# A gated mix of sliding-window attention and a token-mixing MLP on one core: the written order of its five engines is replaced by another order of the same work

## The chip, the cores and the metric

The kernel runs on one core of one Trainium2 chip. The core has five engines that run side by side, each taking its own instructions in order: TensorE (PE, matrix products into the PSUM memory), VectorE (DVE), ScalarE (ACT), GpSimd (POOL) and SyncE (SP), which here only issues DMA transfers. The metric is the time of one execution on the device in microseconds; the number given is the median of several executions.

## The reference

There are 2048 tokens of width 512. Branch A is attention with 32 heads of width 16, in which a token sees itself and the 255 tokens before it. Branch B normalises each token and then mixes tokens: it multiplies along the token axis, 2048 to 1376 and back to 2048, for each of the 512 columns. A gate per token mixes the two.

```python
x = A_x
g = _sigmoid((x * gate_w).sum(-1, keepdims=True))
a = _A_ref(x, A_wqkv, A_wo)
b = _B_ref(x, B_w1, B_b1, B_w2, B_b2)
return g * a + (1 - g) * b

# in _A_ref, H = 32, Dh = 16, W = 256:
scores = jnp.einsum("bhqd,bhkd->bhqk", q, k) * (Dh ** -0.5)
mask = (idx[:, None] - idx[None, :] >= 0) & (idx[:, None] - idx[None, :] < W)
scores = jnp.where(mask[None, None], scores, -1e9)
p = _softmax(scores, axis=-1)
o = jnp.einsum("bhqk,bhkd->bhqd", p, v)
return (lambda x, *d: x.transpose(*d))(o, 0, 2, 1, 3).reshape(B, S, D) @ wo

# in _B_ref, F = 1376:
h = _layernorm(x, axis=-1)
u = jnp.einsum("bsd,sf->bdf", h, w1) + b1
u = _gelu(u)
y = jnp.einsum("bdf,fs->bds", u, w2) + b2
return (lambda x, *d: x.transpose(*d))(y, 0, 2, 1)
```

All inputs and the output are bf16; sums are kept in float32.

## The kernel before

The kernel is written as a list of tasks. A task is one or a few instructions of one engine with a name, the tasks it depends on, and the buffers it takes and uses. The function arrange then puts the tasks into the order in which they are issued. Which engine runs a task, and in which order each engine runs its tasks, is not computed there: it is read from the dictionary PLAN, which holds one written list of task names for each engine. A figure after a colon is the buffer a task takes: a PSUM bank for PE (0 to 7; two figures for a task that takes two pairs of banks), a scratch tile for the others. arrange walks down the five lists, always taking the head task that can start first by its own table of costs (cost_of, TURN, LATENCY). These costs set only how the five lists are woven into one, which projection or MLP product runs in 32-column pieces (the set THEN names tasks after which it does), and where a GpSimd instruction waits for VectorE because of a port that they share. In the program that is built, each engine simply runs its list; between engines there are waits where data or a PSUM bank is handed over.

The names, as PLAN writes them:

- x0.0, x0.2, x1.4, x2.8, x3.12 (line 489): loads of the rows of x, in four blocks of 512 tokens (block 0 in two halves). wqk0 to wqk3 (L505) and wv (L510): the projection's weights. gw (L542): the gate's weights. xt1 to xt3 (L498): loads of blocks 1 to 3 of x that transpose on the way. w1_gi (L521): weights of the first MLP product, group g of columns, tokens of block i. wo (L528), w2_f (L1315): weights of A's last product and of the second MLP product. vs, vz (L756 to L767): copies of V between partitions within SBUF. o0 to o15 (L1343): the output. All are issued by SP, on one queue.
- xta, xtc: block 0 of x transposed by PE (L646) and copied out (L640, L641). warm, warmb: matmuls on zeros ahead of the data (L626).
- k, q, v (all by chain, L708): projections; k2_1.0 is the first piece of K, part 2 of 4, block 1. kc, vc are their copies out of PSUM (ACT L640 or DVE L641), qc the copy of Q with a mask by parity (DVE L792).
- s3.v1, s3.C (L980, L1080, L1036): scores of query block 3. v0 to v3 cover the two key tiles that the window covers mostly, C its two corners. Each needs two pairs of PSUM banks.
- e3.v1.0 (ACT, L932): the exponentials of one of these pairs, 128 x 1024, into a tile et (or into a tile XT, once the transposed x is used up). m3.v1.0: zeros outside the window, by DVE (L1012, L945) or POOL (L571).
- pv3.0 to pv3.3 (L1125): products with V, and with a column of ones for the sum, into a pair of banks. n13, n23, nz3, n33, n43 (DVE, L1216, L1220, L1224, L1233, L1251): the transpose out of PSUM, reciprocal, factor with the gate, product, transpose back into the tile xo, for block 3.
- bs, ba (L808, L812), pow (POOL, L818), h (L824): the layer norm of one tile of 128 tokens. gl, gatem, gatee, ez: the gate.
- u0 to u10 (L708): first MLP product, 16 matmuls each; ub (ACT L473 or DVE L475): bias and copy into ug. gelu (ACT, L1291, L1293): gelu over all of ug at once, with a load of the function table before it, and one of the exponential's after it.
- y0 to y15 (L708): second MLP product and, in the last four matmuls, A's product with wo into the same bank. f (ACT L473, DVE L476) scales and adds the bias, o stores. y15 is cut into three parts l, m, r.

Branches A and B share PE from about 45 us on: u and later y tasks stand between the scores of A, while ACT works on exponentials. A chain of 2 full matmuls is

```python
last = add(
    f"{name}.{a}", {"PE": 0.2155 * sum(m[4] for m in mms[a:z]) / 512}, emit, d,
    takes=[b] if a == 0 else [], uses=([] if a == 0 else [b]) + list(also),
```

so its first piece takes the bank and waits until the last user of that bank has read it.

## Time and profile before

| | us |
|---|---|
| median of 3 runs | 199.56 (199.55 to 199.9) |
| profiled execution | 199.2 |
| its span, first to last instruction | 197.5 |
| TensorE busy | 187.4 (95%) |
| ACT busy | 169.9 (86%) |
| DVE busy | 157.8 (80%) |
| POOL busy | 64.6 (33%) |
| granted TensorE clock | 1.000 |

The profile is of one execution. Times inside it count from its first instruction. A line of the timeline gives the start, the length, the engine, the line of the kernel, the operation, what it writes and reads, how many instructions are merged into the line, and in brackets how long the engine was idle before and what ended that. PEld is TensorE's loading of weights, which overlaps its matmuls. "To landing" is the time from a transfer's issue to the signal that its last byte is there. Matmuls overlap, so the starts of two of them, not their lengths, show the pace.

### The profile page before, as it was taken

To read this page: it belongs to the slowest core of one execution; us is meant where nothing else is said; L and a number is where in the kernel's file an instruction comes from. 1 tells how busy PE (TensorE), PEld (TensorE's weight loads), DVE (VectorE), ACT (ScalarE), POOL (GpSimd) and SP (SyncE) were. 2 spreads that over 40 slices of the span, in tenths; PEclk is the share of its full clock that TensorE was granted. 3 is DMA by queue.
4 is the path that set the end of the run, shared out by engine and by line. 5 is a ranking of instruction groups with operands and counts; after the bars stand their busy time and mean duration, and the time that the engine had idled before them with its cause. 6 is when DMAs were issued, how large, how long until landed. Compare 5 with 4: busy or idle time off the path is not lost.

```text
span 197.5 us, 9026 instructions
## 1 busy us (share of the span) xinstructions
PE 187.4 (95%) x4008; PEld 92.3 (47%) x4040; DVE 157.8 (80%) x340; ACT 169.9 (86%) x200; POOL 64.6 (33%) x102
## 2 busy tenths in 40 slices
...
GB/s 147 306 212 125 236 328 346 317 123 63 7 156 69 275 62 37 0 3 36 134 391 256 3 39 211 0 5 56 3 109 36 27 9 68 3 3 89 3 98 65
DMA packets 23444, 22.01 MB, mean 111 GB/s; under 512 B 7950, under 2 KB 21518, under 8 KB 23406
## 3 DMA queue, kind: packets, MB, share of 16 engines
...
q14 instruction: 7, 0.06, 0.1%
...
## 4 chain that ended last, share of the span: by engine, by line
PE 79%; ACT 11%; DVE 4%; issue 3%; DMA 2%; SPq 0%; ACTq 0%
PE pb L708 57%; PE ps L1125 10%; PE ps L980 9%; ACT et L932 7%; PE ps L1080 2%; ACT VA L640 2%; DMA wqkv<-in_A_wqkv_dram 2%; DVE stats L808 1%; ACT L932 1%; DVE et L1216 1%; DVE zt L1233 0%; SPq L489 0%; ACT ug L1291 0%; DVE h L824 0%; PE ps L1036 0%
## 5 line engine op out<-in xcount | busy, mean ns | idle before, releaser
L932 ACT ACTIVATE et<-ps 128x1024 bf16<-128x1024 f32 (+1 forms) x104 | 98.8, 1011 | 8.2 <-PE ps L980 5.5
L571 POOL TENSOR_SCALAR_AFFINE_SELECT et<-et 128x512 bf16<-128x512 bf16 (+3 forms) x60 | 41.6, 704 | 98.4 <-ACT et L932 65.7
L932 ACT ACTIVATE XT<-ps 128x1024 bf16<-128x1024 f32 (+1 forms) x50 | 49.1, 1028 | 1.2 <-PE ps L980 0.7
L708 PEld LDWEIGHTS <-wb 128*32 128x32 bf16 (+4 forms) x663 | 32.5, 97 | 37.0 <-issue 7.0
L708 PE MATMUL pb<-ug,wb 128*32 128x512 bf16 (+6 forms) x344 | 43.9, 365 | 0.9 <-issue 0.6
L708 PE MATMUL pb<-h,wb 128*32 128x512 bf16 (+2 forms) x301 | 41.9, 380 | 1.7 <-issue 1.7
L708 PE MATMUL pb<-XT,wqkv 128*128 128x512 bf16 (+2 forms) x166 | 31.8, 369 | 1.2 <-issue 0.8
L980 PE MATMUL ps<-QZ,KT 32*128 32x256 bf16 (+1 forms) x496 | 23.1, 265 | 0.9 <-ACT et L932 0.8
L1125 PEld LDWEIGHTS <-VA 128*32 128x32 bf16 (+1 forms) x1056 | 20.3, 97 | 6.2 <-issue 1.6
L792 DVE TENSOR_TENSOR QZ<-pb,par 128x1024 bf16<-128x1024 f32 x16 | 19.1, 1213 | 3.3 <-PE pb L708 2.4
L1125 PE MATMUL ps<-et,VA 128*32 128x128 bf16 (+2 forms) x760 | 21.7, 217 | 0.0
L1216 DVE STREAM_TRANSPOSE et<-ps 128x1024 f32<-128x1024 f32 (+1 forms) x13 | 15.7, 1207 | 4.2 <-PE ps L1125 3.7
L1012 DVE TENSOR_TENSOR et<-et,mask 128x512 bf16<-128x512 bf16 x38 | 16.9, 454 | 2.7 <-ACT et L932 2.7
L708 PEld LDWEIGHTS <-wqkv 128*128 128x128 bf16 (+1 forms) x172 | 12.0, 97 | 13.7 <-DMA wqkv<-in_A_wqkv_dram 0.9
L571 POOL TENSOR_SCALAR_AFFINE_SELECT XT<-XT 128x512 bf16<-128x512 bf16 (+1 forms) x15 | 9.8, 659 | 24.5 <-ACT XT L932 13.5
L708 PE MATMUL pb<-wo,xo 128*32 128x512 bf16 (+3 forms) x152 | 17.5, 369 | 0.4 <-issue 0.3
L980 PEld LDWEIGHTS <-KT 32*128 32x128 bf16 x496 | 7.4, 92 | 21.7 <-ACT et L932 12.1
L708 PE MATMUL pb<-wqkv,XT 128*128 128x512 bf16 x60 | 15.8, 380 | 0.6 <-issue 0.3
L1012 DVE TENSOR_TENSOR XT<-XT,mask 128x512 bf16<-128x512 bf16 x20 | 9.7, 485 | 6.4 <-ACT XT L932 6.4
L808 DVE BATCH_NORM_STATS2 stats<-xo 128x6 f32<-128x512 bf16 x16 | 10.6, 675 | 4.2 <-DMA xo<-in_A_x_dram 4.2
L1125 PEld LDWEIGHTS <-VZ 128*32 128x32 bf16 x832 | 13.2, 97 | 0.4
L1125 PE MATMUL ps<-XT,VA 128*32 128x128 bf16 (+2 forms) x296 | 12.7, 217 | 0.1
...
## 6 DMA issues: line engine op xcount, KB each, us to landing
...
```

The costliest lines, as they stand in the source:

```text
L571: return nc.gpsimd.affine_select(out=out_, in_=in_, pattern=[[0, n] for n in pattern] + [[step, HB]], compare_op=op, fill=0.0, base=base_, ...
L640: return nc.scalar.activation(out_(), in_(), ACT.Copy)
L708: made.append(nc.tensor.matmul(buf(b)[c:z_, c0:c0 + w_], lhsT=lhsT[:, c:z_], rhs=rhs, start=(j == 0), stop=(j == n - 1), skip_group_check= ...
L792: lambda k=k, b=b: nc.vector.tensor_tensor(out=QZ[:, k, :, (i % NQ) * SB:(i % NQ + 1) * SB], in0=buf(b)[:, None, :].to_broadcast([P, 2, SB ...
L808: f"bs{t_}", {"DVE": 0.67}, lambda b=b, t_=t_: nc.vector.bn_stats(buf(b)[:], xo[:, t_, :]),
L932: lambda e=e, b=b, shape=shape: nc.scalar.activation(out=shape(buf(e)), in_=shape(buf(b)), func=ACT.Exp, scale=SCALE),
L980: made.append(nc.tensor.matmul(to[:, :, done:done + m], lhsT=keys(j if x == "A" else j - 1, k)[rows], rhs=q[rows], start=True, stop=True, ...
L1012: made.append(nc.vector.tensor_tensor(out=v, in0=v, in1=m.to_broadcast(list(v.shape)), op=ALU.mult))
L1080: made.append(nc.tensor.matmul(buf(b2[r // 2])[m_:m_ + HB, at:at + P], lhsT=keys(t_, k)[rows, a:a + HB], rhs=q[rows], start=True, stop=Tru ...
L1125: return lambda: nc.tensor.matmul(to(), lhsT=v() if callable(v) else v, rhs=buf(e)[rows, col:col + n], start=first, stop=last, tile_positi ...
L1216: lambda: nc.vector.transpose(out=view(buf(tr).bitcast(FP32)), in_=view(buf(o))), [last], takes=[tr], uses=[o],
```

## The change

All five lists of PLAN and the set THEN are replaced by others. The tasks are the same, 500 on PE and 74 on SP. Those that more than one engine can run are divided anew: ACT's list goes from 194 to 189 tasks, DVE's from 293 to 290, POOL's from 75 to 83. On ACT, ub0, ub1, ub6, ub10, vc13, kc1_1, kc1_2, kc3_3, f9, f12, f15r and one xtc are no longer run, and kc3_2, kc0_1, vc7, vc9, ub4, f10 and another xtc are. Two figures are changed besides: the cost of a score in cost_of, and the latency of the w2 loads, both of which arrange reads. The order was searched outside of the kernel; the description of the change says that this was done in the mean of three sets of durations, with loads and the blocks of TensorE's instructions in one queue of transfers. Nothing of that search is in the kernel.

```diff
@@ -91,7 +91,7 @@
 def cost_of(t, e):
     c, n = t.engines[e], t.name
     if e == "PE":
-        return c - 0.02 if t.mode == "s" else c * 0.738 if t.mode == "c" else c
+        return c - 0.01 if t.mode == "s" else c * 0.738 if t.mode == "c" else c
     if e == "DVE":
         return max(0.1, c - 0.06)
...
 
 PLAN = dict(
     PE="""
-        warm:5 xta0.0.1:4 xta0.0.0:3 warmb xta0.1.1:4 xta0.1.0:5 q2_0.0:6 q3_0.0:0 k1_0.0:2 k3_0.0:3
-        k0_0.0:1 q1_0.0:5 q1_0.1 k2_0.0:7 q0_0.0:4 k2_0.1 q2_0.1 k0_0.1 q0_0.1 k3_0.1 k0_0.2 q0_0.2 k1_0.1
-        q0_0.3 k3_0.2 q1_0.2 k3_0.3 q1_0.3 q3_0.1 q2_0.2 k1_0.2 q1_0.4 k1_0.3 q0_0.4 k0_0.3 k3_0.4 q2_0.3
-        k0_0.4 q3_0.2 q2_0.4 k2_0.2 k1_0.4 k2_0.3 k2_0.4 v1.0:1 q3_0.3 q3_0.4 s0.v0:24 v1.2 v0.0:7 q3_1.0:6
-        v0.2 q3_1.2 s0.C:24 v5.0:0 k2_1.0:7 k2_1.2 v5.2 s-1.C:24 v3.0:6 v14.0:7 v14.2 s1.v3:04 biast:3 v3.2
-        q1_1.0:7 q1_1.2 s1.v0:02 v2.0:6 v2.2 v12.0:4 v12.2 v4.0:5 v4.2 pv-1.0:0 s0.v1:26 k3_1.0:4 k3_1.2
-        k3_2.0:5 s1.v2:06 k3_2.2 v6.0:2 q0_1.0:3 q0_1.2 v6.2 pv0.0:0 pv0.1 pv0.2 s1.v1:46 v7.0:3 v7.2
-        v15.0:2 s2.v1:06 v15.2 k0_2.0:5 v13.0:4 k0_2.2 v13.2 k1_1.0:3 s1.C:06 k2_2.0:2 k2_2.2 k1_1.2
-        s2.v3:06 k0_1.0:5 k0_1.2 v10.0:2 v10.2 pv1.0:0 pv1.1 pv1.2 pv1.3 s2.v0:46 pv1.4 v8.0:2 v8.2 v9.0:3
-        v9.2 s2.v2:06 q2_1.0:5 k1_2.0:4 q2_1.2 s2.C:20 k1_2.2 u0.0:6 u0.2 v11.0:7 v11.2 s3.v1:40 u0.4 u0.6
...
-        u10.4 s8.v1:24 u9.6 u9.8 u10.6 u9.10 s8.v0:20 u9.12 u10.8 u9.14 s8.v2:42 u10.10 pv7.0:0 pv7.1
-        q1_3.0:6 u10.12 u10.14 q1_3.2 s10.v0:24 pv7.2 k2_3.0:7 k2_3.2 pv8.0:2 pv8.1 k0_3.0:6 pv8.2 pv8.3
-        pv7.3 k0_3.2 q2_3.0:4 q2_3.2 q3_3.0:5 y4.0:6 y0.0:7 q3_3.2 s9.v1:02 y0.2 y0.4 y4.2 y4.4 y0.6 y4.6
-        y0.8 y0.10 s9.v3:40 y0.11 y0.13 y4.8 s9.v2:02 y4.10 y4.11 y2.0:7 y2.2 s9.C:40 y2.4 y4.13 y2.6
...
-        y12.8 s15.A:04 y13.4 y13.6 y12.10 y12.11 y13.8 s15.C:02 y12.13 pv14.0:4 pv14.1 pv14.2 s15.B:20
-        y13.10 y13.11 pv14.3 y14.0:6 y14.2 y14.4 y15l.0:1 y13.13 y14.6 y14.8 pv15.0:4 pv15.1 pv15.2 y14.10
-        y15r.0:3 y15l.2 y15l.4 y14.11 y15r.2 y14.13 y15r.4 y15l.6 y15l.8 y15r.6 y15l.10 y15l.11 y15l.13
-        y15r.8 y15r.10 y15r.11 y15m.0:2 y15r.13 y15m.2 y15m.4 y15m.6 y15m.8 y15m.10 y15m.11 y15m.13
+        warm:6 xta0.0.1:7 xta0.0.0:3 warmb xta0.1.0:5 xta0.1.1:4 k3_0.0:1 k1_0.0:2 q2_0.0:3 q0_0.0:0 q2_0.1
+        k0_0.0:7 q0_0.1 q1_0.0:6 k3_0.1 q2_0.2 k1_0.1 q1_0.1 k2_0.0:5 k3_0.2 q0_0.2 q1_0.2 k2_0.1 k0_0.1
+        k0_0.2 k1_0.2 k3_0.3 q1_0.3 q0_0.3 k0_0.3 q0_0.4 k3_0.4 q1_0.4 q3_0.0:4 q2_0.3 k0_0.4 q3_0.1 k1_0.3
+        k2_0.2 q3_0.2 k1_0.4 k2_0.3 k2_0.4 q3_0.3 q3_0.4 q2_0.4 q3_1.0:2 s0.v0:60 q3_1.2 v1.0:5 v1.2 v0.0:4
+        v0.2 s0.C:06 v5.0:3 v5.2 k2_1.0:5 s-1.C:06 k2_1.2 v14.0:4 v14.2 s1.v3:02 v3.0:5 biast:7 v3.2
+        q1_1.0:4 q1_1.2 s1.v0:26 v12.0:5 v2.0:0 v2.2 v12.2 v4.0:1 v4.2 pv-1.0:2 s0.v1:46 k3_2.0:0 q0_1.0:1
+        q0_1.2 s1.v2:62 k3_2.2 k3_1.0:4 v6.0:5 k3_1.2 v6.2 pv0.0:0 pv0.1 pv0.2 s1.v1:26 k1_1.0:5 v7.0:4
+        k1_1.2 s2.v1:60 v7.2 v13.0:2 v10.0:3 v10.2 v13.2 k2_2.0:5 s1.C:06 k2_2.2 k0_2.0:3 k0_2.2 s2.v3:06
+        k0_1.0:4 v15.0:5 k0_1.2 v15.2 pv1.0:2 pv1.1 pv1.2 pv1.3 s2.v0:60 pv1.4 v9.0:5 k1_2.0:4 v9.2 k1_2.2
+        s2.v2:26 v8.0:1 q2_1.0:0 q2_1.2 v8.2 u0.0:2 s2.C:46 v11.0:3 v11.2 u0.2 s3.v1:06 u0.4 u2.0:3 u0.6
+        s3.C:40 u2.2 u0.8 u0.10 u0.12 u0.14 s3.v2:60 pv2.0:4 u2.4 pv2.1 pv2.2 pv2.3 u2.6 u2.8 s3.v0:60
...
+        u9.6 s8.v1:24 u9.8 u9.10 u10.4 u10.6 s8.v0:46 u9.12 u10.8 u9.14 s8.v2:24 u10.10 pv7.0:6 pv7.1 u10.12
+        u10.14 q1_3.0:0 q1_3.2 s10.v0:24 k0_3.0:1 k0_3.2 pv7.2 pv7.3 k2_3.0:4 k2_3.2 pv8.0:2 pv8.1 pv8.2
+        pv8.3 s9.v1:04 q3_3.0:6 q3_3.2 q2_3.0:7 y0.0:2 y4.0:3 q2_3.2 y4.2 y0.2 y0.4 y0.6 y4.4 y4.6 y0.8
+        y0.10 s9.v3:06 y4.8 y0.11 y0.13 y4.10 s9.v2:46 y4.11 y2.0:2 y2.2 s9.C:40 y2.4 y4.13 y2.6 s9.v0:46
...
+        pv13.1 pv13.2 pv13.3 s14.v1:24 y13.0:6 y13.2 y12.0:7 s14.C:40 y13.4 y12.2 y12.4 y12.6 s15.A:24 y12.8
+        y12.10 y13.6 y12.11 y12.13 s15.C:04 pv14.0:2 pv14.1 pv14.2 y14.0:7 pv14.3 s15.B:04 y13.8 y14.2
+        y13.10 y13.11 y14.4 y14.6 y14.8 y13.13 y14.10 pv15.0:4 pv15.1 pv15.2 y15l.0:3 y15l.2 y15r.0:2 y15r.2
+        y14.11 y15r.4 y15r.6 y15l.4 y15l.6 y14.13 y15l.8 y15l.10 y15l.11 y15l.13 y15r.8 y15m.0:1 y15r.10
+        y15r.11 y15m.2 y15r.13 y15m.4 y15m.6 y15m.8 y15m.10 y15m.11 y15m.13
     """,
     ACT="""
-        xtc0.0.1 xtc0.0.0 kc3_0 kc0_0 kc1_0 kc2_0 e0.v0.0:5 e0.v0.1:4 vc0 vc1 e0.C.0:3 e0.C.1:2 kc2_1 vc5
-        e-1.C.1:9 e-1.C.0:8 vc14 e1.v3.0:1 e1.v3.1:b e1.v0.0:a e1.v0.1:0 vc12 gatee0 vc4 e0.v1.1:8 e0.v1.0:9
-        e1.v2.0:6 e1.v2.1:7 kc3_1 vc6 e1.v1.1:2 e1.v1.0:3 e2.v1.1:4 e2.v1.0:5 vc15 kc0_2 e1.C.0:d e1.C.1:c
-        kc2_2 e2.v3.0:8 vc13 e2.v3.1:9 vc10 kc1_1 e2.v0.1:0 e2.v0.0:b vc8 e2.v2.0:1 e2.v2.1:7 e2.C.1:a kc1_2
...
-        e7.v3.1:b e7.C.1:e e7.C.0:7 e7.v2.1:9 e7.v2.0:h e8.v3.1:4 e8.v3.0:5 e8.C.1:c e8.C.0:d e8.v1.0:2
-        e8.v1.1:3 e8.v0.0:0 e8.v0.1:1 gatee3 e8.v2.1:8 e8.v2.0:a ub10 e10.v0.0:6 e10.v0.1:9 gelu e9.v1.0:8
...
-        e14.v1.0:j e14.C.1:5 e14.C.0:e e15.A.0:1 e15.A.1:0 e15.C.0:8 e15.C.1:3 f12:0 e15.B.0:2 e15.B.1:j
-        f13:3 f15r:1
+        xtc0.0.1 xtc0.1.0 kc3_0 kc1_0 kc0_0 kc2_0 e0.v0.1:6 e0.v0.0:7 vc1 e0.C.1:2 e0.C.0:3 vc0 vc5
+        e-1.C.0:9 kc2_1 e-1.C.1:0 vc14 e1.v3.1:8 e1.v3.0:1 e1.v0.0:b e1.v0.1:a vc12 gatee0 vc4 e0.v1.1:0
+        e0.v1.0:9 e1.v2.0:c kc3_2 e1.v2.1:d vc6 kc3_1 e1.v1.1:0 e1.v1.0:9 e2.v1.1:6 e2.v1.0:7 vc7 vc10
+        e1.C.0:4 e1.C.1:5 kc2_2 kc0_2 e2.v3.0:2 e2.v3.1:3 vc15 kc0_1 e2.v0.0:8 e2.v0.1:9 vc9 e2.v2.0:0
+        e2.v2.1:1 vc8 e2.C.1:b e2.C.0:a e3.v1.0:c e3.v1.1:d e3.C.1:e e3.C.0:f e3.v2.1:8 e3.v2.0:9 e3.v0.1:0
...
+        e7.v3.0:3 e7.v3.1:b e7.C.0:a e7.C.1:6 e7.v2.1:4 e7.v2.0:5 e8.v3.1:c e8.v3.0:e e8.C.0:d e8.C.1:f
+        e8.v1.1:8 e8.v1.0:9 e8.v0.0:g e8.v0.1:h e8.v2.0:0 e8.v2.1:1 gatee3 e10.v0.1:2 e10.v0.0:7 gelu
...
+        e14.v1.1:e e14.v1.0:j e14.C.0:a e14.C.1:f e15.A.1:i e15.A.0:7 e15.C.1:8 e15.C.0:9 e15.B.1:d
+        e15.B.0:b f13:3
     """,
     DVE="""
-        zeros bs0:0 ba0 bs3:1 const bs1:0 parity ba3 xtc0.1.0 xtc0.1.1 ba1 bs2:1 ba2 bs5:0 bs6:1 ba5 bs7:0
-        qc0_0 qc1_0 qc2_0 qc3_0 h1 gl3 qc3_1 h2 gl0 h3 ba7 gl1 gl2 biasc vc3 ba6 gatem0 qc1_1 bs4:0 vc2 ba4
-        bs11:1 bs8:0 n1-1:c ez0 ba8 kc3_2 bs10:0 qc0_1 ba10 n10:8 h5 ba11 n20 vc7 bs12:0 n2-1 h6 nz-1:1
-        nz0:0 n3-1:0 bs9:1 h7 m1.v1.0 ba9 n30:1 ba12 bs15:1 kc0_1 bs14:0 m1.C.0 ba14 ba15 bs13:0 ba13 n11:2
...
-        nz12:0 m13.v1.0 m14.v3.0 m13.v2.0 f11:3 n113:2 n312:0 m14.v2.1 m14.v2.0 n213 n412 m14.C.1 m14.v0.0
-        nz13:1 n313:1 m14.C.0 m14.v3.1 n413 m15.A.1 n114:g n214 nz14:1 n314:0 n414 n115:6 n215 nz15:0 n315:1
-        n415 f14:3 f15l:2 f15m:0
+        zeros bs0:1 bs1:0 xtc0.0.0 ba1 parity ba0 bs3:0 bs2:1 xtc0.1.1 ba2 ba3 const bs6:1 bs7:0 ba7 bs5:0
+        ba6 qc0_0 bs4:1 qc1_0 qc3_0 qc2_0 h1 gl7 ba5 h3 qc3_1 gl1 gl0 h0 m-1.C.0 ba4 biasc vc3 gl2 gl3 qc1_1
+        gatem0 vc2 n1-1:4 ez0 bs9:1 ba9 qc0_1 bs14:1 gl8 n10:2 n2-1 bs11:0 ba11 ba14 kc1_1 nz-1:0 n20 h2
+        n3-1:1 nz0:1 bs8:0 bs10:1 h5 n30:0 h6 ba10 vc13 ba8 m1.C.0 m1.C.1 bs15:0 bs13:1 ba15 m2.v3.1 h11
...
+        m13.C.0 n411 n112:g m13.C.1 n212 m13.v2.0 nz12:1 m13.v2.1 f6:2 f11:1 n113:8 n213 m14.v2.1 m14.v0.1
+        n312:1 m14.v0.0 m14.C.0 n412 nz13:0 m14.C.1 n313:1 m14.v1.1 f12:1 n413 n114:2 n214 m15.C.1 nz14:1
+        m15.A.0 n314:1 n414 n115:8 n215 nz15:0 n315:0 n415 f14:2 f15l:3 f15r:1 f15m:0
     """,
     POOL="""
-        ident masks ones blanks pow0 m0.v0.1 m0.v0.0 m-1.C.0 m-1.C.1 m0.C.1 pow1 m1.v3.1 m0.C.0 m0.v1.0
...
+        ident ones masks pow0 blanks m0.C.1 m-1.C.1 m1.v3.0 m0.v0.0 m0.C.0 m0.v0.1 pow1 m0.v1.1 m0.v1.0
+        m1.v2.0 m1.v2.1 m1.v3.1 m1.v0.0 m1.v0.1 m2.v1.0 m1.v1.1 m1.v1.0 pow2 m2.v3.0 m2.v1.1 pow3 m2.v0.1
...
     """,
     SP="""
-        x0.0 x0.2 wqk0 wqk1 wqk2 x1.4 wqk3 gw wv xt1 bias xt3 vs0 x2.8 vs1 xt2 w1_21 x3.12 w1_00 w1_01 w1_10
-        w1_02 w1_20 vs2 w1_23 w1_12 w1_11 vz4:1 w1_03 vz8:0 vz2:2 vz3:2 w1_13 w1_22 vz5:2 wo w2_0 w2_3 vz6:1
-        vz11:2 vz7:1 w2_1 w2_4 w2_2 w2_7 w2_6 w2_5 w2_8 vz10:0 w2_9 w2_10 vz9:1 o2 o4 o7 o0 o8 vz13:1 vz12:0
-        o5 o10 vs13 o1 o11 o9 vz14:1 o13 o3 o6 o12 o14 o15l o15r o15m
+        x0.0 x0.2 wqk0 wqk1 x1.4 wqk2 wqk3 xt1 wv gw xt3 bias x2.8 vs0 xt2 vs1 w1_00 vz2:0 x3.12 w1_01 w1_22
+        wo vs2 w1_12 w1_20 vz6:2 w1_10 w1_03 vz4:1 w1_02 w1_13 vz3:0 w1_21 w1_11 w2_1 w2_2 w1_23 vz5:0 w2_7
+        vz9:1 w2_6 vz8:0 w2_3 w2_5 vz7:2 w2_4 w2_8 w2_0 w2_10 w2_9 o4 vz11:2 vz10:0 o0 o8 o2 vz12:1 o5 o1
+        vs13 vz14:0 o10 o9 vz13:2 o6 o11 o7 o13 o12 o3 o14 o15l o15r o15m
     """,
 )
 
 THEN = set("""
-    pv-1.0 pv0.2 pv1.0 pv1.2 s2.v0 pv2.0 s3.v1 s3.v2 pv3.2 pv3.3 s4.v1 pv4.0 pv4.1 s5.v0 pv5.0 pv5.3 s6.v1
...
+    pv0.1 pv1.2 pv1.3 s2.v0 pv2.0 pv2.2 s3.v1 s3.v2 pv3.0 pv3.1 pv3.3 pv4.0 pv4.1 pv4.2 pv4.3 s5.v0 pv5.0
...
 """.split())
@@ -1312,7 +1311,7 @@
         gone = [piece[f"u{c}.{row // 2 * 2}"] for c in range(4 * g, min(4 * g + 4, NFC))]
         dw2.append(add(
             f"w2_{fc}", {"SP": 1.55 * fsz / P},
-            lambda fc=fc, fsz=fsz: nc.sync.dma_start(w2[:fsz, fc, :], B_w2[fc * P:fc * P + fsz, :]), gone, lat=2.9,
+            lambda fc=fc, fsz=fsz: nc.sync.dma_start(w2[:fsz, fc, :], B_w2[fc * P:fc * P + fsz, :]), gone, lat=3.2,
```

## The prediction

> **What bounds the kernel now.** I read the page's table of engines first, then the chain that ended last, then TensorE's own waits, and last the timeline of single stretches.
>
> ```profile
> PE 187.4 (95%) x4008; PEld 92.3 (47%) x4040; DVE 157.8 (80%) x340; ACT 169.9 (86%) x200; POOL 64.6 (33%) x102
> PE 79%; ACT 11%; DVE 4%; issue 3%; DMA 2%; SPq 0%; ACTq 0%
> ```
>
> TensorE (PE) is busy for 187.4 of 197.5 us and holds 79% of the chain. Matmuls overlap, so busy time alone doesn't say that PE runs at its pace; the starts do.
>
> ```profile
> 54.74 0.40 PE L980 MATMUL ps<-QZ,KT 32*128 32x256 bf16 x8
> 55.07 1.47 PE L708 MATMUL pb<-h,wb 128*128 128x512 bf16 x6
> 56.47 0.40 PE L980 MATMUL ps<-QZ,KT 32*128 32x256 bf16 x8
> 56.80 1.47 PE L708 MATMUL pb<-h,wb 128*128 128x512 bf16 x6
> 58.20 0.40 PE L980 MATMUL ps<-QZ,KT 32*128 32x256 bf16 x8
> ```
>
> Six full matmuls take 1.40 us from start to start (55.07 to 56.47): 6 x 0.216 and one change of tile shape of 0.10. Eight score matmuls take 0.33, 0.23 and another change. These paces hold wherever PE waits for nothing. I took the pace of each kind from the median distance of starts in this trace and added up the whole order of before from its first projection (5.82 us) to its last matmul (start 194.32). The sum is 186.86 us, the trace has 188.50: only 1.64 us of that stretch are waits. The rest of the span is 5.82 of start (limited by the first weights) and 3.17 after the last matmul starts (its output and the final store). So the work is a stream without gaps, and no order of the same work can gain more than about 1.6 us there.
>
> ```profile
> engine line waited for: us in total, times, longest us
> PE pb L708 <- issue: 3.8, 24, 0.2
> ...
> PE ps L980 <- ACT et L932: 0.8, 3, 0.4
> ```
>
> The 24 "issue" gaps are mostly single missing records (4040 weight loads against 4008 matmuls), not time. By starts, the 1.64 us lie at four places: 0.36 before the first scores, 0.83 between 29 and 43 us, 0.73 around 114 to 126, 0.15 at 190; the rest (0.43 back) is where my paces are a little too slow.
>
> **The change, step by step.** All five written lists and the set THEN are replaced. The cost figure of a score in cost_of and the latency of the w2 loads (2.9 to 3.2) only steer where waits for the shared port and tiling are written; they issue nothing.
>
> *Stream.* The same 500 PE tasks stand in the new list. Pieces of 32 columns go from 548 to 574, full ones from 532 to 526, changes of shape from 189 to 191. Two changes are +0.20, the tiled pairs run 0.43 like the full ones. With the paces above, the new order adds up to 187.00: +0.14.
>
> *Start.* In before, wqk2 goes out ahead of x1 (the second block of x); in after, x1 goes ahead of wqk2.
>
> ```profile
> 5.82 3.98 PE L708 MATMUL pb<-XT,wqkv 128*128 128x256 bf16 x25 [0.23 <-DMA wqkv<-in_A_wqkv_dram]
> 9.99 0.81 PE L708 MATMUL pb<-XT,wqkv 128*128 128x512 bf16 x3 [0.19 <-issue]
> ```
>
> Landings in before: wqk0 5.8, wqk1 7.0, wqk2 7.7, x1 9.1, wqk3 9.7. The new order wants wqk1 for its tenth matmul: 9 x 0.109 after 5.82 is 6.80, so it waits 0.25. It wants wqk2 for its 21st: 5 x 0.109 and 6 x 0.216 later, 8.9; with x1 (1.39) ahead, wqk2 lands at 9.1: another 0.25 to 0.3. Together 0.55 against 0.36: +0.19 (ends: 0, if transfers overlap as they do in part, and +0.5). The score that follows needs two query copies, which end on DVE at about 13.5; PE gets there at 13.8, so this lateness isn't hidden there.
>
> *SP's queue.* xt1 is issued before wv and gate_w. The transposing load of before held SP from 5.44 to 12.55, until what was ahead had landed; now only wqk3 is ahead, so it should release SP at about 9.7 and land 2 us later. wv then lands near 13.9 (4.1 us from issue, as wo does), and its first use comes at 14.6: hidden, with 0.7 to spare. gate_w is used at 16. x2 now goes ahead of vs0, but vs0 waits for the V copy that ACT reaches only at 18.4 instead of 16.5, and xt2 is behind it: lands near 23.9 (before: 24.7), first used at 25.6. w1_00 and the copies vz2 go ahead of x3. wo moves up from 63.84 into the stage of loads: 512 KB, about 1.5 us of a full queue. It delays w1_10, w1_03 and w1_02 behind it; I place the last at 44, its use at 49.4: nothing. The w2 loads wait for the same products as before and land earlier than 122.9, at which PE waits 0.12 now; that wait only hands over to the next one, below.
>
> *29 to 43 us.* Here ACT runs without a pause and DVE nearly so, and each wait of PE is for a bank. The first (0.31, value products of block 0) is for two masks on POOL that end at 29.7. The new POOL list ends these at about 29.0, and PE comes at 29.8: gone. The second (0.16) is for DVE's transpose of block 0, then the third and fourth (0.35) for ACT and POOL.
>
> ```profile
> 30.82 1.25 DVE L1216 STREAM_TRANSPOSE et<-ps 128x1024 f32<-128x1024 f32 x1 [0.52 <-PE ps L980]
> ```
>
> The next score, s2.v1, takes the same banks in both orders: in after the transpose could start at 30.55 and end at 31.8, PE wants the banks at 32.03: a margin of 0.1. I take 0.50 of the 0.83 as staying: -0.33 (ends -0.83 and +0.8).
>
> *Gelu, 112 to 126 us.*
>
> ```profile
> 112.93 1.94 ACT L932 ACTIVATE et<-ps 128x1024 bf16<-128x1024 f32 x2
> 114.89 1.28 ACT L1291 ACT_TABLE_LOAD   x1
> 116.18 4.66 ACT L1291 ACTIVATE ug<-ug 128x1536 bf16<-128x1536 bf16 x3
> 120.74 0.61 ACT L1293 ACTIVATE ug<-ug 96x512 bf16<-96x512 bf16 x1
> 121.37 1.28 ACT L932 ACT_TABLE_LOAD   x1
> ```
> ```profile
> 123.75 0.40 PE L980 MATMUL ps<-QZ,KT 32*128 32x256 bf16 x8 [0.38 <-ACT et L932]
> ```
>
> From s10.v0 ACT needs its two exps, a table, gelu, a table and one exp before s9.v3 may have its banks: 11.3 us. PE has 10.56 us of work between the two in after, 10.59 in before. The wait of 0.7 stays whatever else moves: 0.
>
> *Engines beside PE.* ACT has 5 operations fewer (12 handed to DVE, 7 taken), about 3 us of 169.9; DVE 3 fewer, POOL 8 more masks of 0.66. Only a late one costs anything. For new misses I have no row: the lower end is 0 (waits that can go are counted above, so nothing is left to gain), the upper the 1.3 us that the order of before leaves after its start; a few of some hundred meeting points will miss, and margins like those counted (0.1 to 0.7) are larger than most of the scatter that I see between like operations: +0.25.
>
> A row speaks against more masks on POOL: DVE's mask at 143.44 took 1.35 us beside two of POOL's, where the median is 0.42.
>
> ```profile
> 141.94 2.59 POOL L571 TENSOR_SCALAR_AFFINE_SELECT et<-et 64x1024 bf16<-64x1024 bf16 x2 [0.34 <-DVE XT L1012]
> 143.44 1.35 DVE L1012 TENSOR_TENSOR XT<-XT,mask 128x512 bf16<-128x512 bf16 x1
> ```
>
> The Trainium skill says why, in "GPSIMD Engine Reference", section 1 (Specifications): GpSimd's way into SBUF is shared with VectorE, and the two contend when a VectorE instruction reads two SBUF inputs, as a mask does. By that rule each of eight moved masks may stretch a neighbour, and one stretched in front of a value product would put the sum at +1.2 us instead of +0.25. PE shows no wait after 143.44, so I go by the row.
>
> *Tail.* From the last value products of block 15 to the first product that needs them, both orders put the same 2.5 us of PE work; DVE's chain took 2.17 from 190.52 and ended as PE arrived (192.69, 192.75). In after DVE starts it sooner against PE's end. 0 (ends -0.1, +0.3).
>
> Sum: +0.14 + 0.19 - 0.33 + 0.25 = +0.25 us. Span 197.5 to 197.75, profiled execution 199.2 to 199.45. The median shown, 199.56, is 0.36 above the profiled run, so I forecast 199.8.
>
> **Rivals.** 0.2% is 0.4 us, about what a measurement of this kernel can tell from no change.
>
> Same (0.34): the above; its own range is 199.2 to 199.95.
>
> Faster (0.24): the waits of 29 to 43 vanish and no new one appears: 0.14 + 0.19 - 0.83 = -0.5, 199.05; with a start that costs nothing -0.7. For it: the 1.6 us of waits are real, and ACT has 3 us more room. Against it: 0.7 of them (gelu) cannot go.
>
> Slower by the load of x3 (0.20): DVE's list has a statistics step of x3's rows (bs14) directly ahead of block 0's transpose, where before had none so early. If x3 lands after 29.8 rather than at the 29.0 that I place it at, the transpose and s2.v1 move with it one to one; decided from 0.1 us on. Before's x3 landed 5.4 us after its issue; from 24.75 that is 30.1, which makes +0.9, and if vs0 holds SP for 1 us more, +1.9. ACT, without a pause here, would carry the delay on. 200.5 to 201.5.
>
> Slower by scattered misses (0.22): as many as before had of every kind, 1.3 us instead of 0.75 and the dearer start: +0.4 to +1.2, 200.0 to 200.8.
>
> **How the numbers follow.** The likeliest case gives 199.8. Faster than 198.8 needs more than the waits that can go; 201.6 takes in the late x3. About 0.08 and 0.10 stay outside. Faster 0.24, same 0.34, slower 0.22 + 0.20.
>
> **What would show it.** Right: 0.216 a matmul and 191 changes as before; PE's waits by start at 6.8 and 9, none over 0.2 from 29 to 43, and 0.4 to 0.8 ahead of the score after gelu; last matmul 3.2 us from the end. Wrong: PE waiting on DVE's transpose near 32 with a gap "DMA xo" on DVE before it; a wait for wv at 14.6; or a second wait on ACT after 126.

## The result, and the profile after

The changed kernel takes 200.44 us in the median of 16 executions against 199.89 for the kernel before on the same chip (16 executions). The ratio is 1.0037, with a 95% interval from 1.0021 to 1.0053. (The ratio is not the quotient of the two medians, 1.0028. Where executions lie more than 1.5% above the fastest of their kernel, the ratios leave them out and the medians do not; without them the median of again, below, is 200.34 in place of 200.59, and no other moves by more than 0.1.) It is slower, by more than the 0.2% that the prediction set as its bound. The time lies in the forecast range (198.8 to 201.6), but the case forecast as likeliest, no change, did not come.

Later comparisons of the same kernel gave 1.0034 (1.0000 to 1.0067) and 1.0041 (1.0019 to 1.0062). All 40 executions of it have the median 200.59, the 90 of the kernel before 199.64. The difference is 0.94 us; drawing as many executions anew from these, many times over, leaves it between 0.55 and 1.17. It lies inside of the span: the median span of the 40 is 198.65 us, that of the 74 executions of before beside the experiments 197.9.

The page of the changed kernel, first the span, then the engines, then the chain that ended last:

```profile
span 198.7 us, 9080 instructions
PE 187.8 (95%) x4028; PEld 93.0 (47%) x4060; DVE 158.4 (80%) x337; ACT 167.1 (84%) x195; POOL 70.2 (35%) x108
PE 78%; ACT 6%; DMA 5%; SPq 3%; issue 3%; DVE 3%; POOL 1%; ACTq 0%; DVEq 0%
```

PE's busy time is what it was. ACT's share of the chain fell from 11% to 6%, and transfers (DMA) and the sequencer that issues them (SPq) came in, 2% to 8% together. PE's own waits say where:

```profile
engine line waited for: us in total, times, longest us
...
PE ps L979 <- ACT XT L931: 0.7, 1, 0.7
PE ps L979 <- DVE et L1215: 0.6, 1, 0.6
PE pb L707 <- DMA wqkv<-in_A_wqkv_dram: 0.3, 1, 0.3
```

The first is the wait behind the gelu that before has too. The second, for DVE's transpose (L1215 here is L1216 of before), is new at this length: the prediction read 0.16 there. The third is the wait for the first weights, wqk0. The chain of work that ended last runs through the second one (start, length, what):

```profile
25.42 5.16 DMA xo<-in_A_x_dram
30.67 0.50 DVE stats L807
31.28 0.68 DVE junk L859 x2
31.96 1.17 DVE et L1215
33.67 2.70 PE pb L707 x12
```

This is the load of x3, then bs14, then a gate sum (gl8), then n10, the transpose of block 0, and then PE: link for link the rival called "Slower by the load of x3".

With the paces that the prediction took from before, the span splits as follows (us; "waits" are what PE's starts lie behind the sum of paces):

| Part | Before | After | Difference | Forecast |
|---|---|---|---|---|
| First projection starts | 5.82 | 6.53 | | |
| Waits from there to the first scores | 0.36 | 0.20 | with the line above +0.55 | +0.19 |
| Waits from the first scores to 46 us | 0.81 | 0.77 | -0.04 | -0.33 |
| Waits from 46 us to the last matmul | 0.47 | 0.48 | 0 | 0, and +0.25 for new misses |
| Sum of paces | 186.86 | 187.00 | +0.14 | +0.14 |
| Last matmul's start to the end | 3.12 | 3.63 | +0.51 | 0 |

These add up to the 1.2 us between the two spans. But this is one execution of each, and the experiments showed that three of these lines change from execution to execution.

### The profile page after: what moved, and what is told of

The parts are those of the page before. It is cut to its first block, busy times and chain, and to the rows that moved or that the text cites. A ratio compares the mean times of both kernels' runs of the same rounds, so it can differ in the third digit from the quotient of the medians.

```text
span 198.7 us, 9080 instructions
## 1 busy us (share of the span) xinstructions
PE 187.8 (95%) x4028; PEld 93.0 (47%) x4060; DVE 158.4 (80%) x337; ACT 167.1 (84%) x195; POOL 70.2 (35%) x108
## 4 chain that ended last, share of the span: by engine, by line
PE 78%; ACT 6%; DMA 5%; SPq 3%; issue 3%; DVE 3%; POOL 1%; ACTq 0%; DVEq 0%
PE pb L707 57%; PE ps L1124 9%; PE ps L979 9%; DMA xo<-in_A_x_dram 3%; PE ps L1079 3%; DMA wqkv<-in_A_wqkv_dram 2%; ACT ug L1290 2%; ACT et L931 1%; SPq L497 1%; POOL et L570 1%; ACT L931 1%; ACT L1290 1%; DVE et L1215 1%; DVE QZ L791 1%; SPq L756 1%
## 5 line engine op out<-in xcount | busy, mean ns | idle before, releaser
L931 ACT ACTIVATE et<-ps 128x1024 bf16<-128x1024 f32 (+1 forms) x108 | 101.9, 1006 | 10.7 <-PE ps L979 6.4
L570 POOL TENSOR_SCALAR_AFFINE_SELECT et<-et 128x512 bf16<-128x512 bf16 (+2 forms) x60 | 41.9, 708 | 81.0 <-ACT et L931 44.5
L707 PEld LDWEIGHTS <-wb 128*32 128x32 bf16 (+3 forms) x701 | 32.1, 97 | 35.0 <-issue 6.5
L931 ACT ACTIVATE XT<-ps 128x1024 bf16<-128x1024 f32 x46 | 45.6, 1048 | 1.6 <-PE ps L1035 1.1
L707 PE MATMUL pb<-ug,wb 128*32 128x512 bf16 (+5 forms) x384 | 44.1, 368 | 1.3 <-issue 1.1
L707 PE MATMUL pb<-XT,wqkv 128*128 128x512 bf16 (+2 forms) x165 | 32.1, 372 | 1.1 <-issue 0.5
L570 POOL TENSOR_SCALAR_AFFINE_SELECT XT<-XT 128x512 bf16<-128x512 bf16 (+2 forms) x21 | 15.4, 734 | 31.9 <-ACT XT L931 20.4
L1215 DVE STREAM_TRANSPOSE et<-ps 128x1024 f32<-128x1024 f32 (+1 forms) x13 | 15.2, 1167 | 11.1 <-ACT ot L472 4.5
L1124 PE MATMUL ps<-et,VA 128*32 128x128 bf16 (+2 forms) x760 | 20.4, 217 | 0.0
L1011 DVE TENSOR_TENSOR et<-et,mask 128x512 bf16<-128x512 bf16 x33 | 14.4, 446 | 4.1 <-ACT et L931 4.0
L475 DVE TENSOR_SCALAR ot<-pb,c,c 128x512 bf16<-128x512 f32 (+1 forms) x13 | 9.6, 739 | 5.2 <-PE pb L707 5.0
L944 DVE TENSOR_TENSOR et<-et,mask 128x1024 bf16<-128x1024 bf16 (+1 forms) x19 | 12.3, 650 | 0.6 <-ACT et L931 0.5
```

The lines of the kernel that those rows point to most:

```text
L475: return nc.vector.tensor_scalar(out=out_, in0=in_, scalar1=scale, scalar2=bias, op0=ALU.mult, op1=ALU.add)
L570: return nc.gpsimd.affine_select(out=out_, in_=in_, pattern=[[0, n] for n in pattern] + [[step, HB]], compare_op=op, fill=0.0, base=base_, ...
L707: made.append(nc.tensor.matmul(buf(b)[c:z_, c0:c0 + w_], lhsT=lhsT[:, c:z_], rhs=rhs, start=(j == 0), stop=(j == n - 1), skip_group_check= ...
L931: lambda e=e, b=b, shape=shape: nc.scalar.activation(out=shape(buf(e)), in_=shape(buf(b)), func=ACT.Exp, scale=SCALE),
L944: return nc.vector.tensor_tensor(out=v, in0=v, in1=m[:, None, :].to_broadcast([P, n, w]), op=ALU.mult)
L1011: made.append(nc.vector.tensor_tensor(out=v, in0=v, in1=m.to_broadcast(list(v.shape)), op=ALU.mult))
```

## The experiments

My first reading of this table was that the loss lies at the two ends, and that nothing is lost in the middle. The first four runs were made to test that, with the late x3 beside it.

**again: the same kernel once more.** No edit.

> The changed kernel once more, unedited, as the base of the others. Theory: 1.2 us of the 1.2 by which its span (198.7) is longer than that of before (197.5) lie at two ends: the first projection starts at 6.53 and not at 5.82 us (with fewer waits behind it, +0.55 until the first scores), and the last matmul starts 3.7 us ahead of the end of the span and not 3.2 (+0.55); between the two nothing net. If the late start is the order's own (x1 ahead of wqk2), wqk0 lands near 6.5 again and the first scores start late again. If it was chance of that execution, wqk0 lands near 5.8 as before and the span is 0.3 to 0.7 shorter. The tail of 3.7 us and the wait of 0.5 to 0.6 ahead of s2.v1 (33.27 us) should stand in both cases. Ratio to before 1.002 to 1.005.

Its span was 197.5, that of before. Two parts of the 1.2 us were gone: the tail took 3.10 us, and s2.v1 waited for nothing. Not the start: wqk0 landed at 6.65. DVE's and PE's lines of this execution:

```profile
29.90 0.70 DVE L807 BATCH_NORM_STATS2 stats<-xo 128x6 f32<-128x512 bf16 x1
...
31.18 1.25 DVE L1215 STREAM_TRANSPOSE et<-ps 128x1024 f32<-128x1024 f32 x1
```
```profile
32.61 0.40 PE L979 MATMUL ps<-QZ,KT 32*128 32x256 bf16 x8
```

x3 landed at 29.80 here, and bs14 started at 29.90 without a pause, at the end of the copy of Q ahead of it. So the margin that the prediction put at 29.8 is the real one, and x3 lands on both sides of it. My first theory falls in this: the tail that I took for the order's own is an event of some executions, and the middle, which I took for even, holds the cost.

**x3_first: x3 ahead of w1_00 and vz2.**

```diff
-        x0.0 x0.2 wqk0 wqk1 x1.4 wqk2 wqk3 xt1 wv gw xt3 bias x2.8 vs0 xt2 vs1 w1_00 vz2:0 x3.12 w1_01 w1_22
+        x0.0 x0.2 wqk0 wqk1 x1.4 wqk2 wqk3 xt1 wv gw xt3 bias x2.8 vs0 xt2 vs1 x3.12 w1_00 vz2:0 w1_01 w1_22
```

> The changed kernel with one edit of SP's list: x3 goes ahead of w1_00 and vz2. Theory (late x3 holds bs14, that holds block 0's transpose, that holds s2.v1): x3 is issued near 23.6 and not 25.42, lands near 28 and not 30.58, DVE's gap of 0.77 us ahead of bs14 goes, the transpose starts near 30.6 and PE's wait ahead of s2.v1 falls from 0.55 to under 0.1. First rival: PE then only meets waits that before had there (0.12 and 0.23 us, for ACT and POOL), so that of 0.55 only 0.2 to 0.3 is won by 46 us. Second rival: DVE is late there of itself; the wait stays over 0.4. Time against the unedited changed kernel: -0.55 by the theory, -0.25 by the first rival, 0 by the second.

x3 was issued at 23.00 and landed at 27.19; n10 started at 30.85 and s2.v1 waited for nothing. The waits of before at pv1.4 and s2.v2 (0.12 and 0.23) did not come back: the first rival is out. Median 199.52 (12 executions) against 200.59 of the unedited kernel beside it, ratio to before 1.0011 (0.9983 to 1.0038).

**x1_behind: wqk2 ahead of x1 again.**

```diff
-        x0.0 x0.2 wqk0 wqk1 x1.4 wqk2 wqk3 xt1 wv gw xt3 bias x2.8 vs0 xt2 vs1 w1_00 vz2:0 x3.12 w1_01 w1_22
+        x0.0 x0.2 wqk0 wqk1 wqk2 x1.4 wqk3 xt1 wv gw xt3 bias x2.8 vs0 xt2 vs1 w1_00 vz2:0 x3.12 w1_01 w1_22
```

> The changed kernel with wqk2 ahead of x1 in SP's list, as before had it. Theory: x1 ahead costs at the start, since wqk2 landed at 9.42 us (7.71 before); with the old order wqk2 lands near 7.7, and the first scores, at 0.55 us later than before, come 0.2 to 0.5 us sooner. Rival: the start is set by wqk0, which was late (6.49 against 5.77) by chance or by something that this edit leaves; then nothing moves by more than 0.1. x1 lands at 9 to 9.5 either way, and its first user, the statistics on DVE, may wait 0.3 more; that is hidden by the theory. Time -0.2 to -0.5 or 0.

The theory was wrong in what it overlooked. wqk0 and wqk2 did land early (5.82 and 7.94), but x1 came at 9.27 (8.79 in the first profile), and the kernel got slower: 201.16, ratio 1.0091 (1.0056 to 1.0127). Both lists of DVE have statistics of x1 ahead of the copies of Q, but the new one has a fourth (bs4) ahead of the second copy, where before has three; they waited for x1:

```profile
9.36 1.29 DVE L807 BATCH_NORM_STATS2 stats<-xo 128x6 f32<-128x512 bf16 x2 [1.92 <-DMA xo<-in_A_x_dram]
```
```profile
14.65 0.40 PE L979 MATMUL ps<-QZ,KT 32*128 32x256 bf16 x8 [0.78 <-DVE QZ L791]
```

So the first scores waited 0.8 us for a copy of Q. SP was also later: x3 was issued at 26.04, landed at 31.93, and s2.v1 waited 1.75. So this exchange cannot be put back alone; the other lists are laid out for it.

**no_late_block: 18 pairs of short matmuls more, ahead of everything.**

```diff
-    add("warm", {"PE": 2.2}, lambda: warming(5, 512), [kz], takes=[wu], ins=10)
+    add("warm", {"PE": 2.2}, lambda: warming(20, 128), [kz], takes=[wu], ins=10)
...
-            between = add("warmb", {"PE": 0.64}, lambda: warming(3, 256), [t], uses=[wu], ins=6)
+            between = add("warmb", {"PE": 0.64}, lambda: warming(6, 128), [t], uses=[wu], ins=6)
```

> The changed kernel with its warm-up split into shorter matmuls (20 of 128 columns for 5 of 512, 6 of 128 for 3 of 256): the same columns through TensorE, 18 pairs of weight load and matmul more ahead of everything. Theory: TensorE's 32nd block of instructions (16 KB) is fetched at 194.36 to 195.29 us, and while it comes SP's issue of the second last stage of stores takes 0.97 us and not 0.33 to 0.46, so that the last store is issued 0.52 us after its value is written and not 0.03. With 18 pairs more the fetch should come 1 to 3 us earlier, between two stores; the issue takes 0.33 to 0.46, and from the start of the last matmul to the end of the span are 3.2 us and not 3.7: time -0.5. Rival: the tail is long because DVE writes the last three pieces (of before ACT wrote one); then the tail stays at 3.7 and the time too. All other blocks move by 18 pairs as well: up to 0.2 either way.

The tail was 3.10 us, as the theory wanted, but again has 3.10 without any edit, so this alone shows little. The kernel took 203.17, ratio 1.0159 (1.0113 to 1.0205). PE had stopped where nothing was to be waited for. Two of the four places:

```profile
65.11 0.29 PE L979 MATMUL ps<-QZ,KT 32*128 32x256 bf16 x4 [0.43 <-issue]
```
```profile
119.94 1.24 PE L707 MATMUL pb<-XT,wqkv 128*128 128x512 bf16 x5 [1.23 <-issue]
```

The records of the transfers point to the reason. TensorE's instructions come in blocks of 16 KB, about 256 each (32 blocks for the 8122 of the changed kernel). Counting in the list of PE's instructions:

| Block asked for | Landed | PE goes on | Its instruction, counted from a block's start |
|---|---|---|---|
| 62.76 | 63.84 | 65.11 | 177 |
| 75.14 | 76.46 | 77.65 | 173 |
| 117.62 | 118.58 | 119.94 | 171 |
| 178.78 | 180.08 | 181.43 | 161 |

Each time PE stood still until 1.2 to 1.4 us after a block had landed, and each time at the same place within a block. 18 pairs more had moved these places into stretches of 32-column pieces, which use instructions up fastest (0.054 us a pair). In the first profiles of before and of the changed kernel PE stands still at no such place. This is read from the times; no run moved the blocks and nothing else.

**bs14_behind: DVE's statistics step behind the transpose.** The second way to cut the same link, with x3 left late.

```diff
-        gatem0 vc2 n1-1:4 ez0 bs9:1 ba9 qc0_1 bs14:1 gl8 n10:2 n2-1 bs11:0 ba11 ba14 kc1_1 nz-1:0 n20 h2
+        gatem0 vc2 n1-1:4 ez0 bs9:1 ba9 qc0_1 gl8 n10:2 bs14:1 n2-1 bs11:0 ba11 ba14 kc1_1 nz-1:0 n20 h2
```

> The changed kernel with one edit of DVE's list: bs14, the statistics of x3's rows, goes behind n10, the transpose of block 0's sums; SP's list stays, so x3 lands as late as it does (29.8 to 31.9 us in the four executions with this place of x3). Theory: the wait ahead of s2.v1 (0 to 1.73 us in these executions) comes from bs14 standing ahead of n10, and is gone whatever x3 does: n10 starts at 30.6 to 31.0, s2.v1 waits under 0.1. Time like that of x3_first: about 0.5 to 1.0 less than the unedited changed kernel, 199.5 to 200.0 in all, and a narrower scatter. Rival: x3 also holds other work (the other statistics, h12 to h15) and the wait moves to the first products of hidden rows after 46 us; then no gain.

```profile
30.86 1.25 DVE L1215 STREAM_TRANSPOSE et<-ps 128x1024 f32<-128x1024 f32 x1 [0.71 <-PE ps L1124]
32.03 0.65 DVE L807 BATCH_NORM_STATS2 stats<-xo 128x6 f32<-128x512 bf16 x1
```

Now n10 waits for PE, whose sums it transposes, and bs14 runs behind it; s2.v1 waited for nothing, and no wait moved to the products after 46 us. Median 199.51, ratio 0.9992 (0.9965 to 1.002). x3 happened to land at 29.71, so this one profile would have had no wait anyway; the times of the 12 executions (three quarters of them under 199.95) say more.

**x3_behind_w1: the dose.** x3 one load further back.

```diff
-        x0.0 x0.2 wqk0 wqk1 x1.4 wqk2 wqk3 xt1 wv gw xt3 bias x2.8 vs0 xt2 vs1 w1_00 vz2:0 x3.12 w1_01 w1_22
+        x0.0 x0.2 wqk0 wqk1 x1.4 wqk2 wqk3 xt1 wv gw xt3 bias x2.8 vs0 xt2 vs1 w1_00 vz2:0 w1_01 x3.12 w1_22
```

> The changed kernel with x3 one load further back in SP's list, behind w1_01 (a load of 512 KB). w1_01 landed 1.36 us after x3 (31.94 against 30.58). Theory: x3 lands 1.3 us later, at 31 to 32.5, and the wait ahead of s2.v1 grows one to one, to 0.9 to 2.2 us; ACT, which has no pause there, carries it on, and the time is 1 to 1.5 us above the unedited changed kernel's, 201.5. Rival: the lateness is made up again by 46 us; then the time moves by under 0.4.

x3 landed at 33.09, and DVE and PE followed:

```profile
33.18 0.69 DVE L807 BATCH_NORM_STATS2 stats<-xo 128x6 f32<-128x512 bf16 x1 [2.92 <-DMA xo<-in_A_x_dram]
34.39 1.25 DVE L1215 STREAM_TRANSPOSE et<-ps 128x1024 f32<-128x1024 f32 x1
```
```profile
35.79 0.62 PE L979 MATMUL ps<-QZ,KT 32*128 32x256 bf16 x8 [2.73 <-DVE et L1215]
```

The median of four executions was 203.87 (ratio 1.0178, 1.0123 to 1.0232), 3.3 above the unedited kernel and more than the 1 to 1.5 expected. Part of it is x3 itself, 2.5 us later than in the first profile and not 1.3. The rest came behind the wait: 1.4 us were lost between 36 and 39 us, where PE ran at a lower clock. The stretches from 34 to 40 us (length, then busy time and count of PE, PEld, DVE, ACT and POOL, then the granted clock, the DMA share and GB/s):

```profile
34.00:36.00 2.00, 0.21 (x8) 0.17 (x8) 2.00 (x5) 0.00 (x0) 0.00 (x0) 0.83 1.08 319
36.00:38.00 2.00, 2.00 (x12) 0.57 (x5) 1.97 (x8) 1.55 (x2) 0.00 (x0) 0.50 0.69 214
38.00:40.00 2.00, 2.00 (x9) 0.78 (x7) 2.00 (x6) 1.44 (x3) 1.27 (x2) 0.81 0.03 8
```

The shares for 34 to 36 and for 38 to 40 us put half the clock from about 35.3 to 38.8: it fell 2.3 us after PE's last matmul had ended, and PE, back at 35.79, ran at it for about 3 us. After the 1.75 us of x1_behind the clock stayed at 1.00.

Five executions with bs14 ahead of n10 now give a line (us):

| Run | x3 landed | n10 started | s2.v1 waited |
|---|---|---|---|
| again | 29.80 | 31.18 | 0 |
| after_b (below) | 30.34 | 31.65 | 0.49 |
| the first profile | 30.58 | 31.88 | 0.56 |
| x1_behind | 31.93 | 33.52 | 1.75 |
| x3_behind_w1 | 33.09 | 34.39 | 2.73 |

n10 starts 1.3 to 1.6 us after x3 lands, which is bs14 and gl8, and PE's wait grows with it nearly one to one. A sixth, no_late_block, shows what the line hangs on besides: x3 landed at 30.34 and n10 started at 31.65 there too, but s2.v1 waited for nothing, because PE itself got to it only at 33.04 (32.55 in after_b).

**x3_and_gelu and x3_gelu_one: the wait behind the gelu.** x3 first, and PE's scores from s9.v3 on two output tasks later in x3_and_gelu, one in x3_gelu_one.

```diff
-        y0.10 s9.v3:06 y4.8 y0.11 y0.13 y4.10 s9.v2:46 y4.11 y2.0:2 y2.2 s9.C:40 y2.4 y4.13 y2.6 s9.v0:46
-        y2.8 y2.10 y2.11 y2.13 s10.C:60 y8.0:3 y8.2 y8.4 s10.v3:46 y7.0:2 y8.6 y7.2 y7.4 s11.v3:04 y7.6
+        y0.10 y4.8 y0.11 s9.v3:06 y0.13 y4.10 y4.11 y2.0:2 s9.v2:46 y2.2 y2.4 y4.13 s9.C:40 y2.6 y2.8 y2.10 s9.v0:46
+        y2.11 y2.13 y8.0:3 y8.2 s10.C:60 y8.4 y7.0:2 y8.6 s10.v3:46 y7.2 y7.4 y7.6 s11.v3:04
```
```diff
-        y0.10 s9.v3:06 y4.8 y0.11 y0.13 y4.10 s9.v2:46 y4.11 y2.0:2 y2.2 s9.C:40 y2.4 y4.13 y2.6 s9.v0:46
-        y2.8 y2.10 y2.11 y2.13 s10.C:60 y8.0:3 y8.2 y8.4 s10.v3:46 y7.0:2 y8.6 y7.2 y7.4 s11.v3:04 y7.6
+        y0.10 y4.8 s9.v3:06 y0.11 y0.13 y4.10 y4.11 s9.v2:46 y2.0:2 y2.2 y2.4 s9.C:40 y4.13 y2.6 y2.8 s9.v0:46
+        y2.10 y2.11 y2.13 y8.0:3 s10.C:60 y8.2 y8.4 y7.0:2 s10.v3:46 y8.6 y7.2 y7.4 s11.v3:04 y7.6
```

> The changed kernel with x3 first (as x3_first) and TensorE's list edited behind the gelu: from s9.v3 to s11.v3 each block of scores stands two output tasks later, so that s9.v3 has 0.86 us more of work ahead of it. The prediction said that the wait of 0.7 there stays whatever else moves, because ACT's chain of 11.3 us is longer than PE's work. Theory: the scores then come when ACT is ready for them, the wait of 0.74 falls under 0.1, and since ACT idles 0.73 us near 138.3 for the next scores, these come 0.7 earlier: time 0.6 to 0.8 below x3_first, 198.8 to 199.0. Rival: ACT is the limit from 124 to 138 and the wait comes back at s9.v2, s9.C or s10.C: no gain.

> x3 first, and from s9.v3 to s10.v3 each block of scores one output task later on TensorE (two in x3_and_gelu, which waited for an output's eviction before y2.0 and dropped the only task between s11.v3 and pv9.0); the number of instructions is that of x3_first. Theory: the wait of 0.74 ahead of s9.v3 becomes 0.31 and ACT's pause of 0.73 near 138 becomes 0.3, so that 0.4 us are won: 199.1 with x3_first at 199.5, and below before. Rival: the 0.43 come back as waits at s9.v2 to pv9.0, as they did in x3_and_gelu (0.42, 0.16, 0.09 and 0.59): no gain or a loss of up to 0.5.

Two tasks later: the wait at s9.v3 went, and others came. PE waited 0.42 at y2.0 for an output bank, 0.16 at s9.v0 and 0.59 at pv9.0, and the kernel took 201.99 (ratio 1.0103, 1.0061 to 1.0146).

```profile
126.75 0.61 PE L707 MATMUL pb<-ug,wb 128*128 128x512 bf16 x2 [0.26 <-DVE ot L475]
...
137.49 0.57 PE L1124 MATMUL ps<-XT,VA 128*32 128x128 bf16 x16 [0.52 <-ACT XT L931]
```

The edit also left 12 instructions fewer, and PE stood 0.36 us at 111.46 and about 0.4 at 161 for instruction blocks, at the same place within a block as in no_late_block, so its loss is not the reordering's alone. One task later, with the number of instructions kept, the wait at s9.v3 was 0.31 as worked out, but 0.28 came back at pv9.0 and behind it. The median, 199.91 (ratio 1.0022, 0.9996 to 1.0049), is that of x3_first_b (199.89) beside it. So the gains that the two theories hoped for did not come, and the runs bear out the prediction's zero for this place: ACT's chain sets the pace there, and what PE does between only moves the wait.

**before_again: a second profile of before.**

> The kernel before once more, for a second profile: how much of the start and of the tail is chance. In its first profile wqk0 landed at 5.77 us, x3 at 28.64, and 3.12 us lay from the last matmul's start to the end. Theory: wqk0's landing scatters from execution to execution (5.69 to 6.99 in the five with the new kernel's lists), before as after. Rival: with wqk2 ahead of x1 it always lands near 5.8 (5.77 and 5.82 in the two such executions).

wqk0 landed at 5.82 and x3 at 28.80, as in the first. The tail was 3.42, for DVE waited 0.39 for a store to free its tile. From the first scores to 46 us it has 0.35 us less of waits than the first profile, 0.46: PE came to the first scores 0.18 later, and waited less near 29.7 and 32.1. In all eleven profiles with x1 ahead of wqk2, wqk0 landed between 5.69 and 6.99, in ten of them later than in the three with wqk2 ahead (5.77, 5.82, 5.82). The rival has the better of it: the place of x1, a load twice as large as wqk2, mostly delays the weights issued before it.

**after_b, x3_first_b and x3_no_32nd: repeats, and the end of PE's list.** The last edit, on top of x3 first:

```diff
-    s14.v3 pv14.2 pv14.3 s15.B s15.C
+    s14.v3 pv14.2 pv14.3 s15.C
```

> The changed kernel unedited, beside the two that follow on the same chip. In three executions of it and near copies of it that had a profile and x3 in this place, x3 landed at 29.7, 29.8 and 30.6 us and the wait ahead of s2.v1 was 0, 0 and 0.55. Theory: the time is that of before plus 0.1 to 0.3 when x3 is in time, and 0.5 to 2 more in the executions in which it is not; so the fastest are near 199.8 and the scatter is wide (199.8 to above 201), median 200.4 to 200.6.

> x3 ahead of w1_00 and vz2, once more (x3 landed at 27.2 us in its first profile). Theory: no late x3 in any execution; median 0.5 to 1.0 below the unedited changed kernel on the same chip, 199.4 to 199.8, within 0.2% of before. Rival: the 1.1 us by which it was faster the first time were the chance of a few slow executions of the other; then the two medians agree within 0.3.

> x3 first, and s15.B taken out of the set THEN: nine output tasks behind it run untiled, 96 instructions fewer on TensorE. The changed kernel's list has about 50 more than that of before and so asks for a 32nd block of instructions at its end (31 in the two profiles of before); in two of eight profiles that fetch fell on the last stores and the end came 0.55 and 1.7 us later. Theory: without the 32nd block no execution has this; the median falls by 0.1 to 0.4 against x3_first_b and the slowest runs by more. The untiled pieces cost one change of shape (0.1). Rival: the 32nd block comes after the last store in nearly all executions; then nothing changes, or 0.1 is lost.

after_b: 200.64 with a late x3 in the profile (table above). x3_first_b: 199.89 (ratio 1.0031, 1.0004 to 1.0059), x3 at 27.68, no wait at s2.v1; its span was still 198.3, because the 32nd block fell on the last stores. The two differ by 0.75, but with 12 executions each the difference alone is not settled (drawing anew gives -0.4 to 1.2). Taken together, the 40 executions of the unedited kernel have the median 200.59 and the 36 of x3_first, x3_first_b and bs14_behind 199.61: 0.97 less, between 0.55 and 1.25. That is before's 199.64 within 0.3. With x3_gelu_one, which has x3 first and as many instructions, it is 48 executions and 199.72. The ratios to before say it more weakly: 1.0034 to 1.0041 for the unedited kernel and 0.9992, 1.0011 and 1.0031 for the three, in the mean 0.0026 or 0.5 us apart; x3_first_b by itself is not told from the unedited kernel.

How the 32nd block costs time is best seen at SP. The first profile of the changed kernel, and x3_first, whose block came after the end; each shows SP's issues of the last six stores (start, length, what):

```profile
191.21 3.21 SPq L1342 DMA_DIRECT2D out_dram<-ot  x3
194.68 0.97 SPq L1342 DMA_DIRECT2D out_dram<-junk  x1
195.75 0.86 SPq L1342 DMA_DIRECT2D out_dram<-ot  x2
```
```profile
190.22 3.21 SPq L1342 DMA_DIRECT2D out_dram<-ot  x3
193.68 0.33 SPq L1342 DMA_DIRECT2D out_dram<-junk  x1
194.11 0.95 SPq L1342 DMA_DIRECT2D out_dram<-ot  x2
```

In the first the block was fetched from 194.36 to 195.29, and the issue that should take 0.33 us took until 195.65. The last store had its value at 195.70 and was issued at 196.22. The same happened in x3_first_b (tail 3.94), and in x3_and_gelu the block was fetched after the last issue, beside the stores themselves (tail 4.83). These are three of ten profiles of kernels with 8110 or 8122 instructions listed for PE; the other seven have 3.10 to 3.12. That makes 0.3 us in the mean. x3_no_32nd had no 32nd block in its profile and a tail of 3.12, but its median was 200.91 (ratio 1.0047, 1.0018 to 1.0077), not lower, so the theory failed. Its executions lie in two groups, near 199.7 and near 201.1. Its one profile is of the lower group, with x3 at 27.54, so what makes the upper one stays open; how much of the same there is in the unedited kernel's slower executions is not shown.

No kernel tried is faster than before beyond the uncertainty.

## Why the prediction was right or wrong

*What bounds the kernel: right.* PE's paces were the same and the new order's sum of 187.00 fits: in again, 0.64 us of waits on top of it give the distance from first to last matmul.

*SP's queue: the step that failed.* The prediction placed the issue of x3 at 24.75 and its landing at 29.0, 0.8 inside its own bound of 29.8. In three profiles of the unedited kernel it was issued at 25.12 to 25.42 and landed at 29.80, 30.34 and 30.58, 4.6 to 5.2 us after its issue. I had taken 4.3 for the sum and kept the 5.4 of before for the rival alone, although it was the only measured duration for this very load in a full queue. The issue was late by the step that the rival named too: vs0 went out at 18.82 and xt2 behind it held SP to 22.26. The mechanism and the threshold were right: landings at 30.34 and 30.58 made s2.v1 wait 0.49 and 0.56, where one to one from 29.8 gives 0.54 and 0.78. The rival's total, 200.5 to 201.5, takes in the median of the 40 executions (200.59), but in part by luck, for its +0.9 holds 0.25 for new misses that did not come. Its chance, 0.20, was too low: x3 was late in two of the three profiles. The other landings were near the forecast, the last one 2.5 us behind it: xt1 released SP at 9.98 (9.7 forecast), wv landed at 14.11 (13.9), xt2 at 24.39 (23.9), w1_02 at 46.50 (44), and PE waited for none of them.

*29 to 43 us: -0.33 forecast.* pv0.2 waited 0.10 and not 0.31, but not for the reason given: the two masks on POOL, placed at 29.0, ended at 30.11 in the first profile and at 30.08 in again, later than the 29.7 of before, and PE came later too. In an execution with x3 in time nearly all of before's waits are gone: from the first scores to 46 us again has 0.14 us of waits against 0.81, so this stretch was worth -0.67, more than forecast; against the second profile of before (0.46) it is -0.32, against the mean of the two -0.50. With x3 at 30.58 it was worth -0.04 by the first.

*Start: +0.19 forecast.* The first projection's start plus the waits to the first scores was 6.73, 6.71 and 6.58 us in the three profiles of the unedited kernel and 6.36, 6.71, 6.38 and 6.81 in x3_first, x3_first_b, bs14_behind and x3_no_32nd, which start alike: 6.61 in the mean, against 6.18 and 6.35 before, about +0.35 (+0.43 with x3_and_gelu and x3_behind_w1, which start alike too and have 6.88 and 7.09). The mechanism was half right. The wait for wqk2 showed where wqk0 was early (0.76 in x3_behind_w1, which had the same head), but mostly wqk0 itself was late, and that the prediction did not see: it took the transfers ahead of x1 to be untouched by it.

*Gelu: 0.* Right, 0.74 in the profiles, and the two runs above put work into it without a gain.

*New misses: +0.25.* After 46 us there are none. The rule of the Trainium skill that was weighed there ("GPSIMD Engine Reference", section 1) did not show its price: VectorE's 128x512 masks took 446 and 436 ns in the mean against 454 and 485 before, with more masks on POOL beside them, and PE waited for none after 46 us. The row was the better guide.

*Tail: 0.* Right in seven of ten profiles; in three the end came 0.5, 0.8 and 1.7 us later, with the 32nd block on the last stores. (The prediction's 3.17 for before counts from 194.32; the last matmul starts at 194.37, hence 3.12 above.) The prediction named pieces of 32 columns as a cost in time, and not that they are instructions to be fetched.

So without the late x3, and against the mean of the two profiles of before (their tails 3.12 and 3.42, that of the ten 3.41), the terms add up to +0.35 + 0.14 - 0.50 + 0.15, about +0.15, and x3_first, x3_first_b and bs14_behind together measure no difference from before in their medians (-0.04 us, between -0.31 and 0.27). Most of the rest goes with the late x3, since two unlike edits that cut its link both take it away in their medians. Its size stays open: in the profiles the wait is 0 to 0.56 us, the ratios say about 0.5, the medians about 0.9. The executions without a profile may have had x3 later still, or lost time as those of x3_no_32nd did; that is not shown.
